# RWKV-7 recurrence and squared-ReLU FFN: stores of N and first weights on ScalarE's queue, early rounding, work dealt anew

## The chip, the cores and the metric

The kernel runs on one core of a Trainium2 chip. The metric is the device time of one execution in microseconds; several executions are taken and their median is given. The profile is of one further execution.

## The reference

Two stages follow each other. The first is a recurrence over time for each of 4 batches and 8 heads, with a 40x40 state; the second is a feed-forward layer over the 3072 rows that the first one makes.

```
for t in range(S):                       # S = 768
    y[:, :, t] = einsum('bhd,bhde->bhe', rt, state)
    Sa = einsum('bhde,bhe->bhd', state, at)
    state_decay = state * wt[:, :, None, :] - einsum('bhd,bhe->bhde', Sa, bt)
    state = state_decay + einsum('bhd,bhe->bhde', vt, kt)
x = y.transpose(0, 2, 1, 3).reshape(B * S, H * D)        # 3072 x 320
h = maximum(x @ w_in, 0.0)                               # w_in 320 x 2048
out = (h * h @ w_out).astype(float32)                    # w_out 2048 x 320
```

`r, k, v, w, a, b` are float32. The two weight matrices come as float64, and the kernel itself has to round them to float32.

## The kernel before, in words

**Chunks and slots.** Time is cut into 6 chunks of 128 steps; with 4 batches this gives 24 units of work, called chunks 0 to 23 (the batch varies fastest). The main loop has 24 slots. Slot i carries the sequential part (`chain`) of chunk i, and beside it prepares later chunks, so that each slot is a mix of several generators.

**What a chunk goes through.** `early(i)` loads nothing itself: it turns `w` on TensorE (PE), runs the decay scans and two reciprocals on VectorE (DVE), turns `b` and `a`, scales them, stores the decays (`kept_e`), multiplies them into the 128x128 matrices N, which ScalarE (ACT) copies out of PSUM (L373 to L377), and stores pieces of N to DRAM: four to `kept_q` or `kept_d`, and for chunks 2 to 23 `kept_n` and, below chunk 10, two `kept_m`. The buffer of N is single, so the next chunk's copies wait until these stores have read it. GpSimd (POOL) then loads the pieces of one unit of chunks (`take`), inverts them row by row (`solving`, L448 and L450), and stores the result to `kept_t`. `inverses(i)` (the "join") loads it back and, for chunks below 10 (`FINE` units), joins blocks of 32 into the 64-wide inverse T: a turn on DVE (L482), a copy on ACT (L484), a product on PE, a copy (L494), a second product, a copy into T (L501). `rest(i)` makes everything else that the chain of chunk i needs (`turn_k`, `make_a`, `turn_rv`, `make_rv`, `turn_down`, `scale_kb`, `turn_state`). `chain(i)` multiplies with T and N in turn, with a short ScalarE copy between the products (`xr` L619, `minus_x` L630, `xr` L637), and ends with the chunk's output (`tokens`, L669) and the new state.

**Units.** POOL solves chunks in units: 0; 1; 2, 3; 4, 5; 6, 7; 8, 9; 10, 11; and then 12 to 15, 16 to 19, 20 to 23. A unit is taken once all its chunks are prepared.

**The weights.** `fetch_weights(n, queue)` loads a float64 block of w_in or w_out (L249); blocks 0 to 2 go to three wide buffers, and later blocks are fetched when the buffer is free again. `rounding()` is a generator of 54 steps for 26 pieces; steps alternate between ScalarE (L258, L262) and VectorE (L266, L267, L275 to L277). Ten pieces of 512 columns belong to w_in, sixteen of 320 to w_out. The FFN's first product starts when w_in is rounded, its second when all of it is.

**The prologue** is written out by hand: the early parts of chunks 0 to 3 are interleaved with the first solve, with the rest and the first chain step of chunk 0, and with chunk 0's join. `go(gen, n)` runs n steps of a generator with a tick after each.

**Order.** All instructions of one engine, and all DMAs issued by it, run in program order. `store(out, in, steps)` puts a DMA into a line from which `tick()` releases it after so many ticks, on SyncE (SP) by default. `woven` (slots 0 to 3) deals generators over 12 steps; `sorted_slot` (slots 4 to 23) has an order written out by hand, with the FFN (`second`) in it. `ahead` says which chunks are prepared in which slot, `pieces_in` how many pieces are rounded in slots 0 to 3; in slot 4 the last eight steps of rounding run by `halves`. Two lines that the change touches:

```
ahead = {0: (4, 5), 1: (6, 7), 2: (8, 9), 3: (10,), 4: (11, 12), 5: (13, 14)}
pieces_in = {0: (4, TOTAL), 1: (6, TOTAL), 2: (6, TOTAL), 3: (7, TOTAL)}
```

After a pair of chunks, the tokens of some heads are moved between partitions by eight DMAs (`moves`), and `gathered` releases them for the FFN.

Of the kernel before, what the change touches and what calls it, by code (L numbers as in the profile page):

```python
# [17 lines left out]
def kernel(  # L18
# [22 lines left out]
    nc = tc.nc  # L41
    ctx.enter_context(tc.manual_schedule())
    B, H, S, D = r.shape
# [63 lines left out]
    def store(out_, in_, steps=2, queue=nc.sync):  # L107
        later(lambda: queue.dma_start(out=out_, in_=in_), steps)  # L108
# [233 lines left out]
    def early(i, g=None, apart=False):  # L342
# [36 lines left out]
        for half in range(2):  # L379
            for n in range(2):  # L380
                at = half * HC + n * Q
                if i < SMALL:
                    kept, to = kept_q[i, :, half, n], at + Q
                else:
                    u = unit_of[i]
                    kept, to = kept_d[u][i - units[u][0], :, half], (half + 1) * HC
                    kept = kept[:, n * Q * HC:n * Q * HC + Q * (to - at)].rearrange("h (s t) -> h s t", s=Q)
                store(kept.rearrange("h s t -> s h t"), t_[at:at + Q, :, at:to], 1, nc.scalar if g is not None and n else nc.sync)
            if i < SMALL and g is None:
                store(kept_m[i][half], joins(half), 1)  # L390
        if g is None:
            store(kept_n[i], t_[:HC, :, HC:], 1)
        else:
            g["dec"], g["N"] = dec, new("N21", [HC, H, HC], 2)
            nc.scalar.copy(g["N"], t_[:HC, :, HC:])
            g["joins"] = spare("joins", i)
            for half in range(2):
                nc.scalar.copy(g["joins"][half * HC:half * HC + Q], joins(half))
# [169 lines left out]
    def rest(i, g):  # L568
        begin(i, g)
        yield  # L570
        yield
        turn_k(i, g)
        joining = inverses(i, g) if i else iter(())
        if soon(i):
            next(joining, None)
        yield
        make_a(i, g)
        yield
        turn_rv(i, g)
        if i == B:  # L580
            fetch_next(i + 1, "r")
        yield
        decay_state(i, g)
        make_rv(i, g)
        if i and unit_of[i] < FINE:
            next(joining)
        yield
        turn_down(i, g)
        yield
        scale_kb(i, g)  # L590
        turn_state(i, g)
        yield
        yield from joining
        yield
# [9 lines left out]
    def chain(i, g):  # L604
# [71 lines left out]
        if n == GB - 1:  # L676
            t_ = tokens[i // GB]
            for j, row, h, d, m_ in moves:
                at = (h % 2) * DP + d
                store(t_[row:row + m_, j], t_[at:at + m_, h // 2], 1)  # L680
            later(lambda: gathered.add(i // GB), 2)
        yield


# [139 lines left out]

    e0, e1, e2, e3 = (early(i, ready[i]) if i in ready else prepare(i) for i in range(B))
    r0, first_slot = rest(0, ready[0]), chain(0, ready[0])
    go(e0, 3)
    go(e1)  # L830
# [11 lines left out]
    load_early(2)  # L842
    go(e1)
    flush()
    solve(0, {12: lambda: take(1, own)})
    go(r0)
    load_early(3)
# [1 line left out]
    go(e2, 2)  # L849
    load(1)  # L850
    go(first_slot)
    go(e2, 2)
    go(e3, 2)
    go(e2)
# [1 line left out]
    flush()  # L856
    join = inverses(0, ready[0])
    go(join)
    go(e3)
    flush()  # L860
    solve(1, {8: lambda: weights_by(0, nc.gpsimd), 20: lambda: take(2, own)})
    run(r0)
    run(join)
    weights_by(1, nc.sync)
    solve(2, {4: lambda: weights_by(2, nc.gpsimd)})
    for gen in (e0, e1, e2, e3):
        run(gen)
    flush()
# [1 line left out]


    TOTAL = 12
    ahead = {0: (4, 5), 1: (6, 7), 2: (8, 9), 3: (10,), 4: (11, 12), 5: (13, 14)}
    ahead.update({i: (i + 9,) for i in range(6, len(order) - 9)})

    pieces_in = {0: (4, TOTAL), 1: (6, TOTAL), 2: (6, TOTAL), 3: (7, TOTAL)}
    done = set(range(B))
    unit = unit_of[B]


    def woven(i, g, ch):
        jobs = [(ch, 8, 0, TOTAL)]
        made = ahead.get(i, ())
        for j, m_ in enumerate(made):
            jobs.append((prepare(m_), 5, j * 5, TOTAL - 5 * (len(made) - 1 - j)))
        if i:
            ready[i + 1] = {}
            load(i + 1, ready[i + 1])
        jobs.append((rest(i + 1, ready[i + 1]), 9, 2, TOTAL))
        m_, end = pieces_in[i]  # L890
        jobs.append((some(rounded, 2 * m_), 2 * m_, 0, end))
        weave(*jobs)
# [15 lines left out]
    def sorted_slot(i, g, ch):  # L908
# [20 lines left out]
                second.thirds()  # L929
                second.whole()  # L930

        halves = lambda: [next(rounded, None) for _ in range(2)] if not begun else None

        if more:
            begin(j, n)
        step(second.make_quarter, halves, halves)
        step(of(turn_rv), on(one), on(one), halves)
        fetch_next(j + 1, "r")
        step(second.make_quarter, halves)
        step(on(ch), of(decay_state))  # L940
        step(of(make_rv), second.thirds)
        step(on(ch), on(one), on(two), on(two))
# [25 lines left out]
    for i in range(len(order)):  # L968
# [4 lines left out]
        if i < B:  # L973
            woven(i, g, ch)
            n = ready[i + 1]
            n["chain"] = chain(i + 1, n)
            next(n["chain"])
            if i == B - 1:
                fetch_next(i + 2, "v")
                loads(i + 2)  # L980
        else:
            sorted_slot(i, g, ch)
# [37 lines left out]
```

## Time and profile before

| what | value |
|---|---|
| time, median of 3 | 987.36 us (986.25 to 987.77) |
| the profiled execution | 987.0 us, its span 985.3 us |
| PE busy | 875.7 us (89%), 8752 matmuls |
| DVE busy | 485.0 us (49%) |
| ACT busy | 275.5 us (28%) |
| POOL busy | 576.1 us (58%) |
| mean granted PE clock | 0.901 |
| DMA | 104.16 MB in 263431 packets, 246148 of them under 512 B |

The shares are means over stages with different limits. The windows view gives them stage by stage: for each stretch of time its length, the busy time and count of each engine, the granted PE clock, the share of the 16 DMA engines that is busy, and the rate. In a timeline a line reads: start in us, duration in us, engine, source line, operation, output<-input, shapes, count, and in brackets how long the engine sat idle before it and what released it. "SPq" and "ACTq" are the DMA issues on SP's and ScalarE's queues; the duration there is the issue, not the transfer.

Slots can be cut at the ScalarE copy into `xr` (L619), one for each chunk: it is written at 106.81, 156.13, 204.25, 243.42, 291.80, 337.44 and 372.81 us for chunks 1 to 7. For chunk 0 it is written in the prologue (30.91), and its first product with T starts at 65.55.

### The profile page before, as it was taken

How to read it: one execution, taken by the hardware profiler on the slowest of the kernel's cores; microseconds unless marked ns; L12 is line 12 of the kernel's file. 1: busy time of each engine (PE TensorE's matmuls, PEld its weight loads, DVE VectorE, ACT ScalarE, POOL GpSimd, SP SyncE). 2: the span in 40 equal slices, each digit the busy share in tenths (PEclk: the TensorE clock that was granted, in tenths of full speed). 3: DMA queues.
4: the chain of work that ended last, by engine and by line, in shares of the span. 5: the costliest groups of instructions: out<-in, count | busy, mean ns of one | idle time of the engine just before them, and what ended most of it. 6: DMA issues, size and time to landing. Idle time of an engine off the chain costs nothing.

```text
span 985.3 us, 21632 instructions
## 1 busy us (share of the span) xinstructions
PE 875.7 (89%) x8752; PEld 725.8 (74%) x8752; DVE 485.0 (49%) x868; ACT 275.5 (28%) x711; POOL 576.1 (58%) x989
## 2 busy tenths in 40 slices
PE   6447666667897999999999999999999999999998
PEld 4436555556685888888888888888888888887776
DVE  5528775758755454475446655632444423331111
ACT  3132423234323342332223232322222222222111
POOL 4788482836018985999976999959999800000000
PEclk9757565657698999999999999999999999999999
DMA  8987987894667579465588772585404364030000
GB/s 100 143 160 131 191 158 164 171 170 118 91 127 132 100 138 183 92 122 78 97 167 156 124 113 70 102 183 82 66 19 78 82 121 71 14 64 8 14 13 14
DMA packets 263431, 104.16 MB, mean 106 GB/s; under 512 B 246148, under 2 KB 252676, under 8 KB 261924
## 3 DMA queue, kind: packets, MB, share of 16 engines
q1 hardware_dynamic: 259188, 86.39, 50.9%
q0 software_dynamic: 3056, 16.26, 6.9%
q8 instruction: 69, 1.13, 0.5%
q10 hardware_dynamic: 1088, 0.13, 0.1%
q14 instruction: 30, 0.25, 0.1%
HBM read 70.11 MB, written 30.66 MB: 102 GB/s over the span
## 4 chain that ended last, share of the span: by engine, by line
PE 64%; SPq 1%; DVE 1%; DMA 1%; ACT 0%; issue 0%; ACTq 0%
PE ps_f L87 36%; PE ps_w L87 11%; PE ps_c L87 11%; PE ps_w L316 4%; PE ps_c L560 1%; PE ps_c L643 1%; PE ps_w L544 1%; DMA dec<-kept_e 1%; SPq L108 1%; SPq L464 0%; DMA tokens<-tokens 0%; DVE decay L357 0%; DVE state L535 0%; DVE RV L332 0%; ACT N L376 0%
## 5 line engine op out<-in xcount | busy, mean ns | idle before, releaser
L448 POOL TENSOR_TENSOR half_p<-half_n,half_t 128x120 f32<-128x120 f32 (+37 forms) x438 | 255.7, 584 | 84.4 <-DMA half_n<-kept_d 26.5
L450 POOL TENSOR_TENSOR half_t<-half_t,half_p 128x120 f32<-128x120 f32 (+37 forms) x438 | 275.9, 630 | 34.3
L87 PE MATMUL ps_f<-w_out,hid 128*128 128x320 f32 x768 | 217.4, 436 | 0.0
L87 PEld LDWEIGHTS ps_f<-w_out,hid 128*128 128x128 f32 x768 | 142.5, 190 | 54.6 <-issue 0.2
L87 PE MATMUL ps_f<-tokens,w_in 128*128 128x256 f32 x672 | 157.2, 388 | 0.0
L87 PEld LDWEIGHTS ps_f<-tokens,w_in 128*128 128x128 f32 x672 | 126.7, 194 | 17.9 <-issue 1.0
L734 DVE TENSOR_TENSOR hid<-hid 128x512 f32<-128x512 f32 x96 | 88.9, 963 | 50.2 <-ACT hid L727 49.7
L727 ACT ACTIVATE hid<-ps_f 128x512 f32<-128x512 f32 x84 | 50.2, 597 | 96.0 <-PE ps_f L87 96.0
L352 DVE TENSOR_TENSOR_SCAN decay<-ps_w,ones 128x64 f32<-128x64 f32 x88 | 23.8, 271 | 81.5 <-PE ps_w L316 81.5
L669 DVE TENSOR_TENSOR tokens<-ps_c,dec 128x512 f32<-128x512 f32 x24 | 16.5, 688 | 79.3 <-PE ps_c L87 79.3
L87 PE MATMUL ps_w<-decay,bT 40*128 40x128 f32 x352 | 30.0, 308 | 27.0 <-DVE decay L365 27.0
L373 ACT COPY N<-ps_w 128x256 f32<-128x256 f32 x48 | 17.7, 369 | 121.6 <-PE ps_w L87 74.7
L87 PEld LDWEIGHTS ps_w<-decay,bT 40*128 40x128 f32 x352 | 27.6, 213 | 30.2 <-issue 19.1
L510 DVE TENSOR_TENSOR kvT<-ps_w,dec 128x512 f32<-128x512 f32 x24 | 16.5, 688 | 66.9 <-ACT minus_x L630 33.9
L87 PE MATMUL ps_f<-tokens,w_third 64*128 64x256 f32 x336 | 46.9, 385 | 1.5 <-DVE w_out L266 1.5
L332 DVE TENSOR_TENSOR RX<-ps_w,upper 128x512 f32<-128x512 f32 x48 | 30.8, 683 | 32.1 <-PE ps_w L87 31.6
L332 DVE TENSOR_TENSOR RV<-ps_w,upper 128x512 f32<-128x512 f32 x48 | 30.9, 686 | 31.1 <-PE ps_w L87 30.8
L87 PEld LDWEIGHTS ps_c<-xr,T 64*64 64x64 f32 x768 | 30.7, 149 | 20.5 <-issue 15.0
L522 ACT COPY rT<-ps_w 128x512 f32<-128x512 f32 x24 | 14.0, 585 | 108.3 <-PE ps_w L316 108.3
L87 PE MATMUL ps_c<-xr,T 64*64 64x40 f32 x768 | 36.8, 243 | 3.6 <-ACT xr L619 1.6
L357 DVE RECIPROCAL decay<-decay 128x256 f32<-128x256 f32 x22 | 38.2, 1736 | 0.0
L532 DVE TENSOR_TENSOR f<-end,dec 128x4 f32<-128x4 f32 x20 | 5.1, 255 | 66.6 <-DMA dec<-kept_e 66.6
(130 smaller groups left out, 1411.7 us busy)
## 6 DMA issues: line engine op xcount, KB each, us to landing
kept_e<-decay SPq DMA_DIRECT2D x22, 633.8 KB
dec<-kept_e SPq DMA_DIRECT2D x22, 633.8 KB
hid<-in_moe_w_out_dram SPq DMA_DIRECT2D x16, 320.0 KB
half_n<-kept_d POOLq DMA_DIRECT2D x6, 768.0 KB, 10.3
in_w<-in_w_dram SPq DMA_DIRECT2D x24, 160.0 KB
in_ab<-in_b_dram SPq DMA_DIRECT2D x24, 160.0 KB
in_ab<-in_a_dram SPq DMA_DIRECT2D x24, 160.0 KB
in_k<-in_k_dram SPq DMA_DIRECT2D x24, 160.0 KB
```

The lines of the kernel that those rows point to most:

```text
L87: nc.tensor.matmul(o, l_, r_, start=start, stop=True, skip_group_check=True)
L316: nc.tensor.transpose(p_[:, q * 128:(q + 1) * 128], pair(x_, q), ident)
L332: nc.vector.tensor_tensor(t_, p_, over4(upper), Alu.mult)
L352: nc.vector.tensor_tensor_scan(up[:, q, MID + 1:C + 1], wT[:, q, MID:], ones, 1.0, Alu.mult, Alu.mult)
L357: nc.vector.reciprocal(down[:, :, MID + 1:C + 1], up[:, :, MID + 1:C + 1])
L373: nc.scalar.copy(plain, p_[:, ::2])
L448: nc.gpsimd.tensor_tensor(p_, part[:, at:at + m_].unsqueeze(1).to_broadcast([128, n, m_]), t3[:, :n, s:s + 1].to_broadcast([128, n, m_]), ...
L450: nc.gpsimd.tensor_tensor(t3[:, :n, s + 1:], t3[:, :n, s + 1:], p_, Alu.subtract)
L510: nc.vector.tensor_tensor(kT, kT_, down[:, :, 1:C + 1], Alu.mult)
L669: nc.vector.tensor_tensor(t_, y_, g["up"][:, :, :C], Alu.mult)
L727: nc.scalar.activation(h_, p_.rearrange("p f t -> p (f t)"), Act.Relu)
L734: nc.vector.tensor_tensor(h_, h_, h_, Alu.mult)
```

## The change

- `early`: the stores of N are no longer put into the line but issued at once, on ScalarE; only for chunks 0 and 1 does the first of each half's two pieces stay on SyncE.
- The first two weight blocks are fetched by ScalarE's queue, the first ahead of solve 0 and the second after the first chain step; the third by GpSimd inside solve 1. Before, they were fetched by GpSimd in solve 1, by SyncE after chunk 0's join, and by GpSimd in solve 2.
- Eight steps of rounding (four pieces, the last of them without its final two operations) run between the issue of the join's loads and the last step of chunk 3's early part.
- The early part of chunk 4 moves into the prologue: one step ahead of solve 1, three between and after the steps of chunk 0's join; its remaining steps run in slot 0.
- What is left is dealt anew over slots 0 to 5 (`ahead`, `pieces_in`); no rounding is left for slot 4.
- `v` of chunk 5 is fetched with `r` in slot 3 and not at that slot's end. The moves of tokens are released two ticks later.

```diff
-                store(kept.rearrange("h s t -> s h t"), t_[at:at + Q, :, at:to], 1, nc.scalar if g is not None and n else nc.sync)
+                (nc.sync if g is not None and not n else nc.scalar).dma_start(out=kept.rearrange("h s t -> s h t"), in_=t_[at:at + Q, :, at:to])
             if i < SMALL and g is None:
-                store(kept_m[i][half], joins(half), 1)
+                nc.scalar.dma_start(out=kept_m[i][half], in_=joins(half))
         if g is None:
-            store(kept_n[i], t_[:HC, :, HC:], 1)
+            nc.scalar.dma_start(out=kept_n[i], in_=t_[:HC, :, HC:])
...
         if i == B:
-            fetch_next(i + 1, "r")
+            fetch_next(i + 1, "r", "v")
...
-                store(t_[row:row + m_, j], t_[at:at + m_, h // 2], 1)
-            later(lambda: gathered.add(i // GB), 2)
+                store(t_[row:row + m_, j], t_[at:at + m_, h // 2], 3)
+            later(lambda: gathered.add(i // GB), 4)
...
-    e0, e1, e2, e3 = (early(i, ready[i]) if i in ready else prepare(i) for i in range(B))
+    e0, e1, e2, e3, e4 = (early(i, ready[i]) if i in ready else prepare(i) for i in range(B + 1))
...
     flush()
+    weights_by(0, nc.scalar)
     solve(0, {12: lambda: take(1, own)})
...
     go(first_slot)
+    weights_by(1, nc.scalar)
     go(e2, 2)
...
     go(join)
+    go(rounded, 2 * 4)
     go(e3)
     flush()
-    solve(1, {8: lambda: weights_by(0, nc.gpsimd), 20: lambda: take(2, own)})
+    go(e4)
+    solve(1, {8: lambda: weights_by(2, nc.gpsimd), 20: lambda: take(2, own)})
     run(r0)
+    go(join)
+    go(e4)
+    go(join)
+    go(e4)
     run(join)
-    weights_by(1, nc.sync)
-    solve(2, {4: lambda: weights_by(2, nc.gpsimd)})
+    go(e4)
+    solve(2)
...
-    ahead = {0: (4, 5), 1: (6, 7), 2: (8, 9), 3: (10,), 4: (11, 12), 5: (13, 14)}
-    ahead.update({i: (i + 9,) for i in range(6, len(order) - 9)})
-
-    pieces_in = {0: (4, TOTAL), 1: (6, TOTAL), 2: (6, TOTAL), 3: (7, TOTAL)}
-    done = set(range(B))
+    ahead = {0: (5,), 1: (6, 7), 2: (8, 9), 3: (10, 11), 4: (12, 13)}
+    ahead.update({i: (i + 9,) for i in range(5, len(order) - 9)})
+
+    pieces_in = {0: (5, TOTAL), 1: (6, TOTAL), 2: (6, TOTAL), 3: (6, TOTAL)}
+    done = set(range(B + 1))
...
         jobs = [(ch, 8, 0, TOTAL)]
+        if i == 0:
+            jobs.append((e4, 2, 0, 4))
...
-        halves = lambda: [next(rounded, None) for _ in range(2)] if not begun else None
...
-        step(second.make_quarter, halves, halves)
-        step(of(turn_rv), on(one), on(one), halves)
+        step(second.make_quarter)
+        step(of(turn_rv), on(one), on(one))
         fetch_next(j + 1, "r")
-        step(second.make_quarter, halves)
+        step(second.make_quarter)
...
             if i == B - 1:
-                fetch_next(i + 2, "v")
                 loads(i + 2)
```

## The prediction

> **What bounds the kernel now.** I read the windows view first, cut where ScalarE writes a slot's `xr` (106.8, 156.1, 204.3, 243.4, 291.8, 337.4, ... us): one row is one slot.
>
> ```profile
> core 0: us, PE busy (x) PEld busy (x) DVE busy (x) ACT busy (x) POOL busy (x), PEclk, DMA share, GB/s
> 0.00:65.50 65.50, 29.23 (x256) 24.09 (x256) 28.26 (x60) 16.21 (x47) 43.39 (x151) 0.78 0.91 129
> 65.50:106.80 41.30, 30.52 (x332) 26.83 (x332) 30.07 (x55) 14.85 (x41) 33.92 (x97) 0.62 0.84 150
> 106.80:156.10 49.30, 31.46 (x332) 27.69 (x332) 37.60 (x67) 17.75 (x45) 26.24 (x73) 0.60 0.88 172
> 156.10:204.30 48.20, 30.98 (x332) 26.89 (x332) 32.00 (x67) 16.07 (x46) 24.67 (x68) 0.57 0.83 166
> 204.30:243.40 39.10, 27.94 (x325) 24.04 (x326) 29.32 (x63) 14.99 (x40) 24.83 (x68) 0.63 0.75 143
> 243.40:291.80 48.40, 42.34 (x409) 36.34 (x410) 30.63 (x64) 15.70 (x39) 3.38 (x9) 0.80 0.61 106
> 291.80:337.40 45.60, 39.24 (x441) 32.89 (x442) 24.48 (x46) 13.63 (x39) 35.64 (x65) 0.93 0.69 121
> 337.40:372.80 35.40, 35.40 (x429) 29.77 (x430) 17.82 (x34) 13.73 (x39) 31.33 (x53) 1.00 0.70 130
> ```
>
> From slot 6 (337.4) on PE is busy all the time at full clock; time is to be had only in the prologue (to 65.5) and slots 0 to 5. There no engine is full: the slot is a relay of VectorE, PE at 0.6 clock and loads. The timelines of PE show which wait ends last:
>
> ```profile
> 170.15 1.11 PE L316 MATMUL ps_w<-ident,in_k 128*128 128x128 f32 x4 [5.55 <-DMA in_k<-in_k_dram]
> ...
> 177.80 1.08 PE L316 MATMUL ps_w<-ident,in_w 128*128 128x128 f32 x4 [4.53 <-DMA in_w<-in_w_dram]
> ...
> 248.82 1.09 PE L316 MATMUL ps_w<-ident,in_v 128*128 128x128 f32 x4 [4.40 <-DMA in_v<-in_v_dram]
> ...
> 255.31 2.17 PE L87 MATMUL ps_f<-tokens,w_third 64*128 64x256 f32 x7 [1.53 <-DVE w_out L266]
> ...
> 312.80 1.08 PE L316 MATMUL ps_w<-ident,in_w 128*128 128x128 f32 x4 [5.93 <-DMA in_w<-in_w_dram]
> ```
>
> The loads are late because SP's queue issues everything in order. At slot 2's start, in SP's timeline, tokens (5.34 us) and seven stores of N (from 154.83 to 160.97) stand ahead of `in_k` (161.73). VectorE's timeline of the prologue shows the one large hole, 20.34 us before it turns chunk 0's blocks:
>
> ```profile
> 61.49 0.45 DVE L482 STREAM_TRANSPOSE spares<-blocks 128x256 f32<-128x256 f32 x1 [20.34 <-DMA blocks<-kept_t]
> ```
>
> **What the Trainium skill says.** "DMA: Bandwidth & Descriptors", section "Issuing engines are not separate DMA queues": transfers of all issuers run on the same 16 engines, and a second issuer saves sequencer time only. The trace agrees: at 22.2 us two ScalarE stores took 1.89 us beside an SP load of 1.98 us. "TensorE: Matmul & The Clock Gate", section "What's actually happening": the clock is half by default, and full after some 3.4 us of sustained work. Here, too: 0.57 to 0.63 in slots 0 to 3, 1.00 from slot 6; the sixteen `w_in` products after the wait at 312.8 took 5.34 us, those at 328.5 took 3.62.
>
> **The change, part by part** (minus is a gain).
>
> *Stores of N.* Four `kept_q`/`kept_d`, up to two `kept_m` and one `kept_n` go to ScalarE: seven per chunk below 10, five after. Median issues of the same stores on SP: 0.52, 0.59, 0.56 us, and 0.43 for `kept_d`; so 3.8 us for seven, 2.3 for five. They come at once after the copies of N, ahead of what ScalarE does next. At a slot's end that is the join:
>
> ```profile
> 152.07 0.26 ACT L377 COPY N<-ps_w 64x128 f32<-64x128 f32 x1
> 152.35 0.75 ACT L494 COPY spares<-ps_w 32x256 f32<-32x256 f32 x2
> 154.31 0.73 ACT L501 COPY T<-ps_w 32x256 f32<-32x256 f32 x2 [1.20 <-PE ps_w L87]
> 156.13 0.42 ACT L619 COPY xr<-ps_c 128x320 f32<-128x320 f32 x1 [1.09 <-PE ps_c L87]
> ```
>
> L494 follows the last copy at once, PE waits for L494, `xr` for PE: the issues lie on the path. So +3.5 (rounded down, ScalarE's four issues of before had a median of 0.43) at the ends of slots 0, 1, 2 and +2.3 at slot 3's, and about +1 in mid-slot for the other chunk, where rounding queues behind the stores and VectorE for it. Both ends: 0 (the join is late anyway) to 10 us per slot end (seven at 1.46, the longest ScalarE issue seen).
> From slot 6 on there is one chunk per slot to slot 14. In slot 8 the copies end at 435.5; `sd` and two relus end by 437.9, the next thing PE needs is `xr` at 441.65, after 3.69 us of idle. 2.3 us fit: 0 taken, +1 per slot (nine slots) at worst, nothing to gain as PE is full.
>
> *SP relieved.* Some 6 us per chunk leave SP's queue; tokens (two ticks later) go behind the next loads. So the waits shown go: slot 0 its 1.1 for `in_w` and 1.4 of a wait for `kept_n` to free N; slot 1 3.25 of PE's wait for `in_w` at 125.8; slot 2 6.5 of 10.1 (the two above; the data still needs its time on engines that are 0.83 busy); slot 3 3.6 (VectorE's wait for `dec`). Bounds: none of it, or another 4 per slot.
>
> *`v` of chunk 5 fetched one slot earlier.* The 4.40 us at 248.8 go. SP sat idle 7.5 us ahead of 234, so the issue (0.61) costs nothing.
>
> *Four pieces rounded in the prologue.* A 512-column piece is five VectorE operations of 0.68 (3.4 us), a 320-column one 2.5. Four take 13.6 us in program order ahead of L482; the hole is 20.3. They need fetches 0 and 1 (1 MB each), now issued by ScalarE near 24 and 32 us, and landed by about 45 if POOL's 5.8 us from issue to landing grows to twice that. The 2 MB pass over engines that were at a share above 1 from 20 to 51 us, so chunks 2 and 3 come some 2 us later. ScalarE's eight issues (4 us) are hidden by the wait for T until 61. What is late next is chunk 3's N, which now queues on ScalarE behind the rounding: near 54 instead of 51, its stores until 60, just ahead of L484. POOL has its four weight issues moved within a busy stretch, 0.
>
> *Chunk 4's early part in the prologue.* Eight scans, two reciprocals, two products: 1.5+3.4+1.3 = 6.2 us of VectorE, most of it beside the join's PE and ScalarE steps. PE's eight transposes (1.97 at half clock) stand ahead of the join's second product, where it waited 0.75 for ScalarE: +1.2. Blocks land about 1 us sooner, as fetch 0 is out of their way. Prologue in sum +0.5; -1.5 to +5.
>
> *Dealt anew.* Slot 0: one early part out (-6.2), one piece in (+3.4): -2.9. Slots 1, 2: as before. Slot 3: chunk 11 in (+6.2), one piece less (-2.5): +3.7. Slot 4: no rounding, so 1.5 of PE's wait at 255.3 goes, and with both waits gone the clock rises sooner than 262.6; PE worked some 13 us at half clock there, a third of it at full saves 4. Slot 5 prepares one chunk, like slot 6, whose `in_w` was loaded a slot earlier: the wait of 5.93, chunk 13's PE work (2.7) and some 2 at half clock after the wait go. I let it come to slot 6's length, 35.4: -10.2.
>
> Sum by slot: prologue +0.5; slot 0 -2.9-2.5+3.5+1 = -0.9; slot 1 -3.25+4.5 = +1.2; slot 2 -6.5+4.5 = -2; slot 3 +3.7-3.6+3.3 = +3.4; slot 4 -4.4-1.5-4+1 = -8.9; slot 5 -10.2. Total **-16.9**, taken as -16. The profiled run took 987.0 (span 985.3), 0.4 below the median of 987.36; so about **971**.
>
> *POOL* could take the gain back: its solves run without a gap from 286 to 786, and T of chunk 20 was loaded at 790.3, 4.3 us after its solve. But unit 6 (chunks 10, 11) is complete a slot earlier, so that chain starts some 45 us sooner, and then waits for N of chunks 15, 19 and 23, which move with the slots. Units take 136 us, and from N of chunk 23 (633) to the use of T of chunk 20 (793) there are 160. Cost 0.
>
> **The rivals.** (a) *ScalarE becomes the bound*, slower: in slots 0 to 3, with DMA share 0.75 to 0.88, issues stall as the 1.46 us one did. Slot ends then cost 10.2 three times and 7.3, mid-slots 3 each: 50 instead of my 16.8, so -16 becomes +17: about 1004. It decides from an issue of about 1.0 us, where the extra 33 are half reached. Against it: medians of 0.43 to 0.59; for it: SP's mean for `kept_q` is 0.80. Nearer values give 988 to 996. (b) *The work is only moved*: slots 0 to 3 and the prologue lose what slot 4 and 5 win, since the transfers there fill the engines and a relieved SP gains nothing: my 16 us of freed waits outside slots 4 and 5 shrink to 4, so about 983. (c) *Stores hidden*: the join waits for its blocks anyway and slot ends cost nothing: 12.8 us less, 958. (d) The rounding finds its weights late and holds L482: prologue +5 to +10, 977 to 981.
>
> **How the numbers follow.** Mine 0.42, (b) 0.15, (c) 0.13, (d) 0.12, (a) 0.18, half of it above 994. Range 955 to 994: it leaves out the bad half of (a) and the edge of (c). A difference under 0.2% (2 us) is about what a measurement of this kernel can't tell from none. Faster 0.77, same 0.06 (between b and a), slower 0.17.
>
> **What would show it.** Right: `in_k`, `in_v`, `in_w` waits of PE gone from slots 2, 4, 5; slot 5 near 36; four roundings between 40 and 60; ScalarE DMA issues between L377 and L494 of 2 to 4 us; PE full from slot 5. Wrong: slot ends with 6 us or more of ScalarE issues; L482 later than 63; PE idle after 337 beside POOL or `xr`.

## The result and the profile after

The change made the kernel slower: **1019.34 us median (1015.64 to 1020.8, 4 runs)** against 987.57 us for the kernel before (4 runs), a ratio of **1.032 (1.0286 to 1.0351)**. The profiled execution, the shortest of the four, took 1015.64 us; its span is 1013.9: 28.6 longer than before, where I had forecast 16.9 shorter.

The windows view of the kernel after, cut at the same events as before's (first product with T, then each `xr` at L619), has one row for the prologue and one for each of slots 0 to 5:

```profile
core 0: us, PE busy (x) PEld busy (x) DVE busy (x) ACT busy (x) POOL busy (x), PEclk, DMA share, GB/s
0.00:85.30 85.30, 32.15 (x269) 26.14 (x269) 45.69 (x90) 20.42 (x55) 46.92 (x160) 0.76 0.85 142
85.30:135.10 49.80, 29.79 (x320) 25.99 (x320) 28.64 (x50) 16.73 (x43) 30.11 (x90) 0.57 0.67 141
135.10:188.80 53.70, 31.80 (x332) 27.93 (x332) 32.99 (x67) 16.05 (x46) 26.57 (x73) 0.60 0.70 143
188.80:236.00 47.20, 31.79 (x332) 27.85 (x332) 31.70 (x67) 15.67 (x46) 22.93 (x64) 0.57 0.75 147
236.00:282.90 46.90, 34.34 (x353) 29.81 (x354) 31.60 (x67) 15.82 (x45) 24.76 (x68) 0.57 0.66 113
282.90:331.10 48.20, 38.76 (x409) 33.70 (x410) 24.36 (x45) 12.98 (x32) 36.28 (x69) 0.88 0.60 119
331.10:366.60 35.50, 35.50 (x429) 29.86 (x430) 20.11 (x36) 13.70 (x40) 31.73 (x49) 1.00 0.58 103
```

The prologue is 19.7 us longer and slot 0 8.6; slot 5 is as short as forecast. The work is the same over the span (VectorE 485.5 us against 485.0, ScalarE 275.5 in both); VectorE's 17.4 us more in the prologue are chunk 4 and the four pieces moved into it. The DMA engines were less busy in slots 0 to 3 than before (0.67, 0.70, 0.75, 0.66 against 0.84, 0.88, 0.83, 0.75). So what grew is waiting. The first fence is from VectorE's list of waits up to 135 us, the next three from PE's in slot 0, in slots 1 to 3, and in slots 3 and 4 (total us, times, longest); the last is from PE's list for slots 1 to 3 of the kernel **before**:

```profile
DVE ps_f L277 <- ACT w_in L262: 17.5, 1, 17.5
```
```profile
PE ps_c L87 <- ACT xr L637: 5.9, 1, 5.9
PE ps_w L87 <- ACT spares L494: 4.4, 1, 4.4
```
```profile
PE ps_w L87 <- DVE decay L365: 21.3, 6, 4.5
PE ps_w L87 <- ACT spares L494: 20.5, 3, 9.9
```
```profile
PE ps_w L316 <- DMA in_w<-in_w_dram: 8.9, 1, 8.9
```
```profile
PE ps_w L87 <- DVE decay L365: 14.5, 3, 6.0
PE ps_w L316 <- DMA in_w<-in_w_dram: 7.8, 2, 4.5
PE ps_w L316 <- DMA in_k<-in_k_dram: 6.0, 2, 5.6
PE ps_w L87 <- ACT spares L494: 5.7, 3, 2.1
```

PE's waits for `in_k` and `in_w` in slots 1 to 3 (6.0 and 7.8 us before) are gone, as forecast; but PE's three waits for the join's copy L494 there grew from 5.7 us to 20.5, and those for VectorE's L365 by 6.8. Most of what grew waits for ScalarE, which has no more work than before. Its timeline in the prologue shows what holds it. "ACTq" are its DMA issues; where a line merges several (x2, x4), the second number runs from the start of the first to the end of the last, with what lies between:

```profile
29.26 2.67 ACTq L249 DMA_DIRECT2D w_out<-in_moe_w_in_dram  x2
31.96 0.59 ACT L522 COPY rT<-ps_w 128x512 f32<-128x512 f32 x1 [7.83 <-DMA kept_q<-N]
...
38.78 10.35 ACTq L249 DMA_DIRECT2D w_out<-in_moe_w_in_dram  x4
49.23 0.37 ACT L373 COPY N<-ps_w 128x256 f32<-128x256 f32 x1 [10.03 <-DMA in_b<-in_b_dram]
...
50.99 0.33 ACTq L388 DMA_DIRECT2D kept_q<-N  x1
...
55.86 0.35 ACTq L388 DMA_DIRECT2D kept_q<-N  x1
57.83 0.67 ACTq L390 DMA_DIRECT2D kept_m<-N  x1
58.59 1.24 ACTq L388 DMA_DIRECT2D kept_q<-N  x2
65.67 0.57 ACTq L390 DMA_DIRECT2D kept_m<-N  x1
66.33 0.57 ACTq L392 DMA_DIRECT2D kept_n<-N  x1
66.95 0.66 ACT L262 ACTIVATE w_in<-w_out 128x512 f32<-128x512 uint32 x1 [15.43 <-DMA kept_q<-N]
```

Read the releasers in brackets: an ordinary copy (L522, L373) is "released" by a DMA whose data it never touches. The issue that stands ahead of the copy was waiting for that DMA. The issues themselves are short up to here, 0.3 to 0.7 us, but **between** them are holes. A semaphore is a counter that an instruction can wait for. The trace names for each DMA the semaphore that it counts up when it lands, when it landed, and what its issue waits for. In this kernel SyncE and ScalarE draw theirs from the same eight semaphores. Each of the prologue's seven long holes stands ahead of an issue that waits for the very semaphore that it will count up, and ends 0.021 to 0.022 us after the landing of the transfer that had it last:

| issue by ScalarE | hole before it, us | its semaphore was last taken by |
|---|---|---|
| weights, 29.26 | 5.12 | a piece of the same weight block, ScalarE |
| weights, 31.62 | 2.07 | `kept_q`, SyncE |
| weights, 43.98 | 4.77 | `in_r`, SyncE |
| weights, 48.83 | 4.16 | `in_b`, SyncE |
| `kept_q`, 55.86 | 4.33 | `in_ab`, SyncE |
| `kept_m`, 57.83 | 1.62 | `kept_e`, SyncE |
| `kept_m`, 65.67 | 5.84 | `blocks`, SyncE |

That is 27.9 us in which ScalarE, which works in order, could start nothing else. In slots 0 to 3 such holes come to no more than 1.1, 1.8, 0.4 and 0.6 us. There the issues themselves stand ahead of the join: from a slot end's first store to L494 it is 4.2, 8.7, 4.7 and 3.3 us. ScalarE's timeline at the end of slot 1:

```profile
176.29 0.31 ACTq L388 DMA_DIRECT2D kept_q<-N  x1
...
177.82 2.56 ACTq L388 DMA_DIRECT2D kept_q<-N  x2
180.42 2.16 ACTq L390 DMA_DIRECT2D kept_m<-N  x1
184.42 0.55 ACTq L392 DMA_DIRECT2D kept_n<-N  x1
185.01 0.75 ACT L494 COPY spares<-ps_w 32x256 f32<-32x256 f32 x2 [8.19 <-DMA kept_q<-N]
```

One hole of 1.84 us is in it, but two issues alone take 1.68 and 2.16. The fourteen of slot 1 take 12.8 us and those of slot 2 10.2, against 7.2 in slot 0; what makes some of them long was not settled.

In the prologue, L522 comes at 31.96 (24.11 before), chunk 2's copies of N at 49.23 (36.65), the first rounding at 66.95, chunk 0's turn L482 at 78.79 (61.49) and its first product with T at 85.3 (65.6).

### The profile page after: what moved, and what is told of

It reads as the page before. It is cut to its first block, busy times and chain, and to the rows that moved or that the text cites. A ratio compares the mean times of both kernels' runs of the same rounds, so it can differ in the third digit from the quotient of the medians.

```text
span 1013.9 us, 21580 instructions
## 1 busy us (share of the span) xinstructions
PE 877.5 (87%) x8752; PEld 728.0 (72%) x8752; DVE 485.5 (48%) x868; ACT 275.5 (27%) x711; POOL 576.1 (57%) x985
## 4 chain that ended last, share of the span: by engine, by line
PE 74%; DVE 8%; DMA 6%; ACT 3%; ACTq 3%; issue 2%; POOL 2%; SPq 1%; DVEq 0%; POOLq 0%
PE ps_f L87 39%; PE ps_w L87 14%; PE ps_c L87 13%; PE ps_w L316 5%; ACTq L388 1%; DMA kept_q<-N 1%; DVE decay L357 1%; PE ps_c L643 1%; DMA blocks<-kept_t 1%; PE ps_c L560 1%; DMA in_w<-in_w_dram 1%; PE ps_w L544 1%; ACT N L376 1%; DVE ps_f L275 1%; SPq L108 1%
## 5 line engine op out<-in xcount | busy, mean ns | idle before, releaser
L87 PEld LDWEIGHTS ps_f<-tokens,w_in 128*128 128x128 f32 x672 | 125.6, 192 | 17.5 <-issue 1.0
L734 DVE TENSOR_TENSOR hid<-hid 128x512 f32<-128x512 f32 x96 | 90.5, 979 | 50.2 <-ACT hid L727 49.7
L727 ACT ACTIVATE hid<-ps_f 128x512 f32<-128x512 f32 x84 | 49.1, 599 | 82.5 <-PE ps_f L87 82.5
L332 DVE TENSOR_TENSOR RV<-ps_w,upper 128x512 f32<-128x512 f32 x48 | 30.9, 685 | 63.1 <-PE ps_w L87 63.0
L87 PE MATMUL ps_w<-decay,bT 40*128 40x128 f32 x352 | 32.1, 326 | 27.9 <-DVE decay L365 24.4
L87 PEld LDWEIGHTS ps_w<-decay,bT 40*128 40x128 f32 x352 | 29.6, 231 | 30.8 <-issue 16.8
L87 PE MATMUL ps_w<-rT,kvT 40*128 40x128 f32 x384 | 33.0, 317 | 17.4 <-ACT kvT L523 14.3
L373 ACT COPY N<-ps_w 128x256 f32<-128x256 f32 x48 | 17.7, 368 | 105.3 <-PE ps_w L87 90.4
L87 PE MATMUL ps_f<-tokens,w_third 64*128 64x256 f32 x336 | 45.6, 378 | 0.5 <-ACT hid L727 0.5
L332 DVE TENSOR_TENSOR RX<-ps_w,upper 128x512 f32<-128x512 f32 x48 | 30.8, 684 | 30.3 <-PE ps_w L87 29.7
L420 POOL DMA_DIRECT2D half_n<-kept_q x14 | 7.3, 528 | 66.4 <-DMA kept_q<-N 39.3
L522 ACT COPY rT<-ps_w 128x512 f32<-128x512 f32 x24 | 14.0, 585 | 108.3 <-PE ps_w L316 100.4
```

The lines of the kernel that those rows point to most:

```text
L87: nc.tensor.matmul(o, l_, r_, start=start, stop=True, skip_group_check=True)
L332: nc.vector.tensor_tensor(t_, p_, over4(upper), Alu.mult)
L373: nc.scalar.copy(plain, p_[:, ::2])
L522: nc.scalar.copy(g["rT"], p_)
L727: nc.scalar.activation(h_, p_.rearrange("p f t -> p (f t)"), Act.Relu)
L734: nc.vector.tensor_tensor(h_, h_, h_, Alu.mult)
```

## The experiments

**Theory 1:** a ScalarE DMA waits for the landing of whichever transfer last had its semaphore, SyncE's included, and holds ScalarE's copies behind it. **Theory 2:** transfers fill the DMA engines, so that issues are slow. **Theory 3:** the rounding ahead of L482 makes the prologue long. Below, T0 is the first product with T and "slots" are slots 0 to 5 of the profiled execution, us:

| run | T0 | slots 0 to 5 |
|---|---|---|
| before | 65.6 | 41.3 49.3 48.1 39.2 48.4 45.6 |
| after | 85.3 | 49.9 53.7 47.2 46.9 48.2 35.4 |
| `w_pool` | 82.7 | 58.5 52.0 46.8 45.9 48.5 36.1 |
| `stores_sp` | 77.4 | 44.0 45.4 47.7 44.7 47.2 35.4 |
| `w_pool_stores_sp` | 71.3 | 49.7 44.3 47.4 44.1 48.4 35.4 |
| `deal_only` | 61.4 | 44.3 50.2 50.3 45.7 56.3 35.4 |
| `before_act_stores` | 59.9 | 60.5 54.3 47.2 38.3 49.2 40.8 |
| `act_stores_later` | 82.7 | 46.8 45.0 56.1 44.6 50.0 35.5 |
| `v_and_tokens` | 62.3 | 45.4 50.1 49.6 39.2 47.7 45.8 |
| `stores_sp_load13` | 75.3 | 41.4 44.2 48.4 45.2 38.1 35.4 |
| `no_rounding_ahead` | 84.8 | 52.4 59.7 47.6 47.6 48.5 36.1 |
| `stores_sp_load13_no_ahead` | 74.9 | 40.4 48.1 48.6 45.2 39.6 35.4 |
| `weights_pool_load13` | 68.6 | 56.9 43.3 47.7 44.9 39.3 35.4 |
| `deal_load13_v_tokens` | 61.3 | 45.3 51.3 49.3 45.4 46.3 35.4 |

Executions of the same prologue differ: before, `deal_only`, `v_and_tokens` and `deal_load13_v_tokens` have T0 at 65.6, 61.4, 62.3 and 61.3. Single stages are read to 2 to 4 us only. The ratios below are to the kernel before measured beside each run, with medians of 989.64 to 989.91 us.

**`stores_sp`** is the change with the stores of N back in SyncE's line.

```diff
-                (nc.sync if g is not None and not n else nc.scalar).dma_start(out=kept.rearrange(...), in_=...)
+                store(kept.rearrange(...), ..., 1, nc.scalar if g is not None and n else nc.sync)
-                nc.scalar.dma_start(out=kept_m[i][half], in_=joins(half))
+                store(kept_m[i][half], joins(half), 1)
-            nc.scalar.dma_start(out=kept_n[i], in_=t_[:HC, :, HC:])
+            store(kept_n[i], t_[:HC, :, HC:], 1)
```

> The changed kernel, but the stores of N go back to SP's queue with their old delay; weights still by ScalarE. Theory 1: the 15.4 us that ScalarE stood between the copies of chunk 2's N and its first rounding go, so the prologue shortens by 10 to 15 us (first product with T at 70 to 75), and each of slots 0 to 3 loses the ScalarE issues at its end (4.4 us of PE's wait in slot 0, up to 9.9 and 6.2 in slots 1 and 2): time 985 to 995. Theory 2: only the slot ends change, prologue stays at 85: 1000 to 1008. Theory 3: as theory 2.

985.95 us, ratio to before 0.9972 (0.9945 to 0.9998). This one edit takes back the whole loss: 25.4 us between the profiled spans, some 34 by the two ratios (the change's profiled execution was its shortest, this one's 4.2 above its median). Prologue and slots 0, 1 and 3 give it (7.9, 5.9, 8.3, 2.2). ScalarE still stands for 17.5 us in five holes ahead of weight issues.

**`before_act_stores`** is the converse: the kernel before with only those stores at once on ScalarE.

> The kernel before, with only the stores of N moved to ScalarE and issued at once. Theory 1 (a ScalarE store waits for the landing of the transfer that last used its completion semaphore, and what ScalarE does next waits behind it): clearly slower, by 8 to 30 us: each of slots 0 to 2 longer by 3 to 10 us, the prologue by up to 10, and ScalarE's DMA issues show gaps that end within 0.1 us of such a landing. Rival (issue time alone, 0.5 us each): 3.8 us per slot end, 10 to 15 us in all, without gaps. If the stores are harmful only together with the weights and the rounding ahead: within 5 us of before.

1006.73 us, ratio 1.0165 (1.0131 to 1.02). Slot 0 grows from 41.3 to 60.5. PE's list of waits from 60 to 250 us (slots 0 to 3) again names ScalarE:

```profile
PE ps_w L87 <- ACT spares L494: 19.9, 3, 9.6
PE ps_w L87 <- ACT kvT L523: 12.6, 3, 10.2
PE ps_c L87 <- ACT xr L637: 7.6, 3, 6.7
```

Here there are no weights on ScalarE and no new rounding, so neither is needed for a loss, and the holes are there: 10.1 us of them in slot 0. But T0 is 59.9: ahead of it nothing is lost, so what the change loses there needs the weights, too. Slot 6 alone is 9.2 us longer (44.6 against 35.4): a store `kept_d` stands 4.9 us for its semaphore, the copy into T (L501) comes behind it, and PE waits for that:

```profile
365.46 1.04 PE L87 MATMUL ps_c<-xr,T 64*64 64x40 f32 x16 [3.38 <-ACT T L501]
```

In the 14 us after it PE's granted clock is 0.63; before, it is 1.00 in all of slot 6.

**`act_stores_later`** keeps the stores on ScalarE, but releases them from the line a tick later instead of at once.

```diff
-            nc.scalar.dma_start(out=kept_n[i], in_=t_[:HC, :, HC:])
+            store(kept_n[i], t_[:HC, :, HC:], 1, nc.scalar)
```
(and so for `kept_q`, `kept_d` and `kept_m`)

> The changed kernel, but the stores of N, still on ScalarE, go through the line with a delay of one tick, so that they come behind what ScalarE does in the same step (join, rounding). If the order at the slot ends is what costs (L494 behind seven stores): 8 to 15 us less than the changed kernel, 1004 to 1011, with PE's wait for L494 back under 3 us. If the waits for semaphores cost wherever the stores stand: the prologue still has its first product with T at 80 or later, and the time falls by less than 8 us: 1011 to 1019.

1015.65 us, ratio 1.0247 (1.0204 to 1.0291). Some slots gain and slot 2 loses 9; T0 is still 82.7. PE's waits for L494 are down to 5.7 us from 60 to 250 us, but it waits for other copies of ScalarE instead (L637 9.4, L523 8.2, L619 7.6). By the ratios 7 of the 34 us come back: it is the engine that issues, more than the place in the slot, that costs.

**`w_pool`** and **`w_pool_stores_sp`** give the first two weight blocks to GpSimd; the second also takes the stores of N back to SyncE.

```diff
-    weights_by(0, nc.scalar)
-    solve(0, {12: lambda: take(1, own)})
+    weights_by(0, nc.gpsimd)
+    solve(0, {4: lambda: weights_by(1, nc.gpsimd), 12: lambda: take(1, own)})
...
-    weights_by(1, nc.scalar)
```

> The changed kernel, but GpSimd issues weight blocks 0 and 1 (block 0 at the same place ahead of solve 0, block 1 at step 4 inside solve 0). Theory 1: in the prologue ScalarE stands still at its own DMA issues, because each waits until an earlier transfer that uses the same completion semaphore (101 to 108, shared with SP) has landed. GpSimd uses eight others (111 to 118), so ScalarE's waits of 5.1, 2.1, 4.9 and 4.2 us between weight issues go, rT is written near 25 us instead of 32, the copies of chunk 2's N near 38 instead of 49. The stores of chunk 2's N still wait, so the first product with T moves from 85.3 to 68 to 74, and the time from 1019 to 1003 to 1008. Theory 2 (the 2 MB crowd the DMA engines, whoever issues them): prologue and time stay within 3 us. Theory 3 (rounding and chunk 4's early part simply stand ahead of the join): stay, too.

> Both: weights 0 and 1 by GpSimd and stores of N on SP; rounding ahead, chunk 4's early part in the prologue, the new deal, v and tokens stay as in the changed kernel. Theory 1: no DMA of ScalarE is left but four; the prologue is back to 65 to 68, slot 5 stays at 35.5: time 970 to 980, below the kernel before. Theory 2: 2 MB still in the prologue, first product with T at 75 or later, time over 988. Theory 3: rounding holds the turn of chunk 0's blocks: first product with T at 72 or later.

1019.85 us, ratio 1.031 (1.0285 to 1.0334), and 991.13, ratio 1.000 (0.9987 to 1.0012). Both are misses: I had expected T0 at 68 to 74 and at 65 to 68, and nothing lost elsewhere. With the weights gone ScalarE copies chunk 2's N earlier (44.65 in `w_pool`), but its stores still have holes (47.01 to 59.52 for seven), and the blocks come late. GpSimd now issues before it solves (chunk 0's result is stored at 57.21, in the change at 48.19), and SyncE's loads of it, four issues, take 13.44 us. The first fence is SyncE's timeline, the second ScalarE's:

```profile
61.86 13.44 SPq L470 DMA_DIRECT2D blocks<-kept_t  x4
```
```profile
77.59 0.91 ACT L484 ACTIVATE T<-blocks,which 128x256 f32<-128x256 f32 x2 [7.40 <-DMA blocks<-kept_t]
```

The second of the four stands 10.70 us and goes out at 73.27, 0.016 us after ScalarE's store `kept_q` of 69.65 has landed, which had its semaphore. So SyncE, too, is held by a transfer of the other engine that it shares no data with, here right ahead of T0. Theory 2 had expected `w_pool` within 3 us of the change, in T0 and in time, and so it is; but what holds T0 there is this wait, not slow issues.

In `w_pool_stores_sp` T0 falls by 6.1 beside `stores_sp`, and slot 0 gives 5.7 back: PE waits 9.9 us for `in_w` there, and ScalarE 10.5 for `kept_n` to free N. What the weights cost on ScalarE comes back in slot 0 when GpSimd issues them.

**`no_rounding_ahead`** is the change with no rounding ahead of the join (theory 3).

```diff
-    go(rounded, 2 * 4)
-    pieces_in = {0: (5, TOTAL), 1: (6, TOTAL), 2: (6, TOTAL), 3: (6, TOTAL)}
+    pieces_in = {0: (6, TOTAL), 1: (7, TOTAL), 2: (7, TOTAL), 3: (7, TOTAL)}
```

> The change without the four pieces rounded ahead of chunk 0's join (they go to slots 0 to 3). Theory 1 (waits for semaphores hold ScalarE's copies): VectorE turns chunk 0's blocks once they have landed, near 68 instead of 78.8, chunk 0's first product with T comes at 74 to 76 instead of 85.3; slots 0 to 3 get 1 piece each more, +1.5 to 3 each; total 1012 to 1018: of the prologue's 19.7 us some 10 are the rounding that was held by late stores, the others ScalarE's own waits. Theory 3 (the rounding alone makes the prologue long): the first product comes by 66 and the total is under 1008. If the weights' and stores' waits hold the blocks anyway, the first product stays past 82 and the total at 1019.

1024.5 us, ratio 1.0352 (1.0327 to 1.0376); T0 84.8. L482 did come early, at 69.67, but ScalarE's next step of the join did not. Its timeline:

```profile
73.27 0.37 ACT L373 COPY N<-ps_w 128x256 f32<-128x256 f32 x1 [21.04 <-DMA kept_n<-N]
...
78.88 1.74 ACTq L390 DMA_DIRECT2D kept_m<-N  x1
80.71 0.71 ACTq L392 DMA_DIRECT2D kept_n<-N  x1
81.47 0.91 ACT L484 ACTIVATE T<-blocks,which 128x256 f32<-128x256 f32 x2 [5.91 <-DMA kept_q<-N]
```

Chunk 2's last store of N went out only at 69.11, so chunk 3's copies waited 21 us for the buffer, and its seven stores stand ahead of L484. Theory 3 falls, and so does my own split of the prologue: of the alternatives on record the last held. In the change two chains end together, the rounding (L482 at 78.79) and chunk 3's stores (L484 at 81.97 right behind them), and both begin after chunk 2's late stores.

**`deal_only`** is the kernel before with the new `ahead` alone, **`v_and_tokens`** with `v` and the tokens alone.

```diff
-    ahead = {0: (4, 5), 1: (6, 7), 2: (8, 9), 3: (10,), 4: (11, 12), 5: (13, 14)}
-    ahead.update({i: (i + 9,) for i in range(6, len(order) - 9)})
+    ahead = {0: (4, 5), 1: (6, 7), 2: (8, 9), 3: (10, 11), 4: (12, 13)}
+    ahead.update({i: (i + 9,) for i in range(5, len(order) - 9)})
```

> The kernel before with the deal alone: chunk 11 prepared in slot 3, chunks 12 and 13 in slot 4, one chunk per slot from slot 5 on; prologue, stores, weights and rounding as before. If the prediction's step for the deal was right: slot 5 from 45.6 to about 35.5, slot 3 longer by 4 to 8, slot 4 shorter or the same: time 978 to 985. If the wait of PE for in_w only moves from slot 5 to slot 4 (the changed kernel shows one of 8.9 us there): 985 to 990.

> The kernel before, with v of chunk 5 fetched in slot 3 and the moves of tokens two ticks later, nothing else. The prediction's step: PE's wait of 4.4 us for in_v in slot 4 goes, waits for in_k in slot 2 shrink: 978 to 985. If another load is late in its place: 985 to 990.

993.75 us, ratio 1.0042 (1.0027 to 1.0056), and 988.17, ratio 0.9977 (0.9965 to 0.9989). The dealing takes 10.2 from slot 5 and gives 6.5 to slot 3 and 7.9 to slot 4: a slightly slower kernel. PE waits 3.4 us for `in_w` in slot 3 and 8.0 in slot 4. The early `v` removes its wait of 4.4 from slot 4, but PE's wait for the rounding there (L266) grows from 1.5 to 4.8, and only 2 us of time come of it.

**`stores_sp_load13`** asks whether slot 4's loss is only that load: `stores_sp`, and chunk 13's `w`, `b` and `a` loaded at the end of slot 3.

```diff
             if i == B - 1:
+                load_early(3 * B + 1)
                 loads(i + 2)
```

> The changed kernel with the stores of N on SP (as in stores_sp) and, in addition, the inputs of chunk 13 loaded at the end of slot 3 and not when slot 4 starts to prepare chunk 12. PE's wait of 8.9 us for in_w in slot 4 should go: slot 4 from 47.2 to 39 to 41 and the time from 986 to 977 to 980. If slot 4 is bound elsewhere (VectorE, clock), 2 us or less come.

**979.37 us, ratio 0.9884 (0.9852 to 0.9915)**: faster than both kernels, and by one line faster than `stores_sp`. Its windows view for slot 4 and PE's list of waits from 225 to 331 us:

```profile
254.50:292.60 38.10, 37.88 (x411) 33.10 (x410) 22.93 (x46) 12.87 (x32) 13.44 (x34) 0.95 0.85 168
```
```profile
PE ps_w L316 <- DMA in_w<-in_w_dram: 2.0, 1, 2.0
```

Slot 4 falls from 47.2 to 38.1 at a clock of 0.95, with PE nearly always busy: the 9.9 us that I had forecast for its dealing were there, behind one late load.

**Three versions around it.** `stores_sp_load13_no_ahead` also drops the rounding ahead; `weights_pool_load13` gives the weights to GpSimd inside the solves and rounds two pieces ahead; `deal_load13_v_tokens` is the kernel before with the dealing, `v`, the tokens and the early load, its prologue untouched.

```diff
 weights_pool_load13, beside stores_sp_load13
-    weights_by(0, nc.scalar)
-    solve(0, {12: lambda: take(1, own)})
+    solve(0, {12: lambda: take(1, own), 20: lambda: weights_by(0, nc.gpsimd)})
-    weights_by(1, nc.scalar)
-    go(rounded, 2 * 4)
+    go(rounded, 2 * 2)
-    solve(1, {8: lambda: weights_by(2, nc.gpsimd), 20: lambda: take(2, own)})
+    solve(1, {8: lambda: weights_by(1, nc.gpsimd), 20: lambda: take(2, own)})
-    solve(2)
+    solve(2, {4: lambda: weights_by(2, nc.gpsimd)})
-    pieces_in = {0: (5, TOTAL), 1: (6, TOTAL), 2: (6, TOTAL), 3: (6, TOTAL)}
+    pieces_in = {0: (6, TOTAL), 1: (6, TOTAL), 2: (6, TOTAL), 3: (7, TOTAL)}
```

> The stores of N in SyncE's line, chunk 13's w loaded a slot early, and no rounding ahead of the join. If the rounding ahead pays even with the stores back (it fills VectorE's hole), this is slower than 979 by the work that slots 0 to 3 get: 982 to 988. If the rounding is what keeps the first product with T at 75 instead of 62 to 66, the prologue falls by 5 to 10 and slots 0 to 3 gain 6 to 10: 975 to 982, no difference that matters.

> The stores of N in SyncE's line, chunk 13's w loaded a slot early, the weight blocks issued by GpSimd inside the solves of chunks 0, 1 and the next unit, two pieces rounded ahead. Theory 1: with no 1 MB block issued by ScalarE no long wait stands ahead of its copies, the first product with T comes at 63 to 68 (75.3 with the blocks on ScalarE), slots 0 to 3 get 1 piece more in three of them (+1.5 to 3 each): 968 to 977. If GpSimd's late issue makes the rounding wait for its data and hold VectorE's turn of the blocks, the prologue stays at 72 to 76 and the total at 980 to 986.

> The kernel before with the new dealing of chunks (chunk 11 in slot 3, 12 and 13 in slot 4, one a slot from 5 on), v of chunk 5 and the tokens as in the change, and chunk 13's w loaded a slot early; prologue, weights, rounding and stores of N as before. If the parts add up: the dealing alone was 4.0 us slower than before, the early w takes the wait of 8 us for it (and some 6 at half clock) from slot 4, v another 4: 974 to 982. If PE's waits in slots 3 and 4 only move to what is late next (ScalarE's and VectorE's relay), 984 to 990.

981.67 us (ratio 0.992, 0.9896 to 0.9945), 983.71 (0.9943, 0.9927 to 0.9958) and 981.95 (0.9918, 0.9895 to 0.9942). Without the rounding ahead T0 is 74.9 instead of 75.3: the four pieces do lie in VectorE's hole at no cost once the stores are off ScalarE, but what they save is small. T0 stays near 75 with the weights still on ScalarE. Chunk 2's copies of N are late by it, SyncE's stores of N follow them, and the join's loads stand behind these in SyncE's queue: issued at 62.06 in `stores_sp_load13_no_ahead` and at 54.34 before, though the solve had ended by 49.5 in both. `weights_pool_load13` clears that (T0 68.6) but rounds on data that have not come. In slot 0 VectorE waits for a weight block, and PE for VectorE, as their lists of waits up to 130 us show:

```profile
DVE ps_f L275 <- DMA hid<-in_moe_w_in_dram: 16.6, 1, 16.6
```
```profile
PE ps_w L316 <- DVE A L332: 16.6, 1, 16.6
```

Slot 0 is 56.9, and the total misses the 968 to 977 that I had hoped for. `deal_load13_v_tokens` has most of the gain with the old prologue: in sum the rearranged prologue is worth little or nothing (the intervals of 0.9918 and 0.9884 overlap). What pays differs. There it is mostly slot 5, with 10.2 us; slot 4, still with rounding in it, is 46.3, and PE waits 4.8 us for L266. Where no rounding is left in slot 4, it is 38.1 and 39.6, and that makes up for the longer prologue.

**The wait by itself.** In `count_of_eight` and `ninth_transfer` nothing of the reference is computed. They have seven stages of loads, of which this is the core (`ninth_transfer` also has ScalarE copy something first):

```
for m_ in range(count):                       # loads of 1 MB
    loads_by.dma_start(out=big[m_], in_=rows[...])
small_by.dma_start(out=small, in_=...)        # one load of 10 KB
```

> No part of the reference is computed: seven stages, each of K loads of 1 MB by one engine and then, by another engine and with nothing in the data to wait for, one load of 10 KB. Pairs: SyncE 4, 7, 8, 10 then ScalarE; GpSimd 8 then ScalarE; SyncE 8 then GpSimd; SyncE 8 then ScalarE. Theory 1 (SyncE's and ScalarE's transfers take eight completion semaphores in turn): with 4 and 7 ScalarE's load is issued at the stage's start; with 8 it is the ninth and is issued within 0.1 us after the stage's first 1 MB load has landed, 5 us or more into the stage; with 10 after the third has landed; behind GpSimd's loads, and by GpSimd behind SyncE's, at once. Theory 2 (a ScalarE issue is slow when the DMA engines are full): the issue is stretched in all stages alike, growing with K, behind GpSimd's loads too.

> No part of the reference is computed: seven stages, each begun when everything of the stage before has landed. In each, one engine issues K loads of 1 MB; ScalarE copies for about 4 us and then issues one load of 10 KB into a tile that nothing else has touched. SyncE with K = 12, 4, 8, 10, 12; then GpSimd with K = 12; then SyncE with 12. Theory 1: with 4 ScalarE's load goes out right behind its copies; with 10 and 12 behind SyncE's it goes out later, within 0.1 us after a load of SyncE's has landed, the one that last used its semaphore; behind GpSimd's 12 it goes out right behind the copies. SyncE's own ninth load waits for its first in the same way. Theory 2 (full DMA engines slow the issue itself): it goes out right behind the copies each time and takes longer, with 12 of either engine.

The first tested nothing on ScalarE: from its second stage on, the small load overwrote a tile that VectorE still had to read, so it was not free to go. The second showed the sharing, from the other side. SyncE's list of waits from 70 to 113 us, in stages whose buffers had all been free since the stage began:

```profile
SPq L59 <- DMA big<-in_moe_w_in_dram: 10.7, 7, 2.3
SPq L59 <- DMA small<-in_r_dram: 1.7, 2, 1.0
```

SyncE's load of its own 1 MB tile waits for **ScalarE's** 10 KB load, which it shares nothing with but a semaphore: the two go out at 79.54 and 108.35, 0.016 us after the small load has landed. Within a stage of 12, SyncE's later loads wait for its own first ones in the same way (0.017 us after their landings). GpSimd's loads from the ninth on wait for GpSimd's own first ones, on eight other semaphores. ScalarE's load itself never waited, which I had expected with 10 and 12: it went out some 2.7 us into the stage, and its semaphore had been free for 15 us or more. With four to ten of the 1 MB loads issued ahead of it its issue took 0.47 to 0.54 us, so a busy DMA alone did not slow it; the long issues of slots 1 and 2 in the change are left unexplained. The test did not force a hole on ScalarE. That ScalarE's holes are such waits is read in the traces of the full kernels, from what each issue waits for and when that landed; what they cost, from `stores_sp` and `before_act_stores`.

## Why the prediction was wrong

Two steps failed. The prediction put the waits ahead of ScalarE's issues at nothing, and the prologue took 19.7 us more instead of 0.5; and it took the relief of SyncE as a gain of 15.85 us in slots 0 to 3, where no gain is to be seen. `stores_sp` splits the difference in two, between profiled executions. The stores' part is the cost on ScalarE less the relief of SyncE; the rest is everything else:

| | stores, forecast | stores, measured | rest, forecast | rest, measured |
|---|---|---|---|---|
| prologue | 0 | +7.9 | +0.5 | +11.9 |
| slot 0 | +2.0 | +5.9 | -2.9 | +2.7 |
| slot 1 | +1.25 | +8.3 | 0 | -3.9 |
| slot 2 | -2.0 | -0.5 | 0 | -0.4 |
| slot 3 | -0.3 | +2.2 | +3.7 | +5.5 |
| slot 4 | +1 | +1.0 | -9.9 | -1.2 |
| slot 5 | 0 | 0 | -10.2 | -10.2 |
| from slot 6 | 0 | +0.7 | 0 | -1.2 |
| sum (measured: of the spans) | +2.0 | +25.4 | -18.8 | +3.2 |

By the medians the stores' part is some 34 us and the rest -2.8 (ratio 0.9972).

- **Stores of N: wrong.** The step "3.8 us for seven" priced each DMA by its issue. By their medians the issues were as priced (0.47, 0.46, 0.59 and 0.53 us for `kept_q`, `kept_d`, `kept_m`, `kept_n`), and slot 0's end shows it well: seven stores from 127.15 to 131.31, L494 at 131.36. Missing is the wait ahead of an issue. In the prologue seven stores took 15.9 us, and in the sum I gave them nothing there. At the ends of slots 0 to 3 there are few such waits: 20.9 us instead of 12.8, most of the difference in slot 1, where issues were long. Rival (a) had the direction, and 1004. Its long issues are there in part (a mean of 0.91 us in slot 1, 0.73 in slot 2), but the prologue's loss, which it did not have, comes of holes of up to 5.8 us between short ones. (Its 16.8 us of mine count four mid-slots; my sum by slot has five, 17.8. Nothing hangs on it.)
- **SyncE relieved: the waits went, the gain was wrong.** The waits for `in_k` and `in_w` in slots 1 to 3 went, 13.8 us; PE's waits for L494 there grew by 14.8, and those for L365 by 6.8. A load that comes sooner was worth nothing where the join came later. With the stores back on SyncE (`stores_sp`) those waits for loads are there again, 13.7 us, and slots 0 to 3 are 15.9 us shorter.
- **Weights in the prologue: wrong.** "now issued by ScalarE near 24 and 32 us, and landed by about 45": they were issued until 49.1. I asked when the data come, and not what ScalarE could do meanwhile. With the weights on ScalarE and the stores back, T0 is 75 to 77, with neither of them there 71.3, before 61 to 66. ScalarE issued four DMAs in the trace of before, too few to show it. Such a wait in SyncE's queue is in that trace, and I had not looked for it: at 65.29 us a weight issue follows a hole of 1.81 and the landing of a `kept_q` by 0.016.
- **The Trainium skill's sentence was read too widely.** "DMA: Bandwidth & Descriptors", section "Issuing engines are not separate DMA queues", promises a saving of sequencer time to a second issuer. No run here contradicts that of SyncE; what it costs the engine that issues is not in it. The two long issues at 22.2 us that I read as agreement show only that two issues can be long at once.
- **Rounding ahead: right only with the stores off ScalarE.** Then it fits VectorE's hole at no cost (T0 75.3 with it, 74.9 without).
- **Slot 4: wrong.** `v` and the rounding step went as forecast (4.4 and 1.5 us of PE's waits gone), and the clock rose. But the wait for `in_w` that I took out of slot 5 came back in slot 4, with 8.9 us: chunk 13 is now prepared there, and its `w` is loaded only when chunk 12 is begun. I had looked for the wait where one chunk is left and not where the second one went. `stores_sp_load13` removes it, and slot 4 gives 10.3 beside before.
- **Slot 3: mis-sized.** I set +3.7 for chunk 11 (less one piece) against -3.6 for VectorE's wait for `dec`. That wait fell to 0.9 in `deal_only` and to nothing in `stores_sp` and in the change. But the slot got 6.5 longer in `deal_only` and 5.5 in `stores_sp`: the sum had VectorE's work for chunk 11 in it, but not PE's, which was busy 3.5 and 6.6 us longer there at a granted clock of 0.65 and 0.58. New are also waits of VectorE for PE's products (L332), 4.7 and 3.8 us. No single one of these accounts for the slot.
- **Slot 5, slots from 6 on and POOL: right.** 45.6 to 35.4 as forecast, for the reason given; from slot 6 on 647.4 us against 647.9. That the stores cost nothing there is in part luck: in `before_act_stores` one of them meets a taken semaphore, and slot 6 loses 9.2. (GpSimd's solves before were not "without a gap": from 286 to 786 us it waits 26.5 for its own loads. The conclusion stands.)
- **Left open.** Why some issues of slots 1 and 2 are long. And slot 0 of `stores_sp` is +2.7 and not -2.9. Up to there `stores_sp_load13` is the same program, and had 41.4 instead of 44.0, so most of this may be the spread between executions.

## What to carry to other kernels

A DMA moved to another engine costs that engine the issue and every wait that stands ahead of it. Where two engines draw on the same completion semaphores, each can be held by a slow transfer of the other (ScalarE for 22.8 of its 27.9 us in the change's prologue, SyncE for 10.7 in `w_pool`), and a compute engine that works in order holds all its copies meanwhile. Look in the timeline for ordinary copies released by a DMA whose data they do not read. When work is dealt anew, follow each load to the slot where its user now stands: one line that issued a load a slot earlier took `stores_sp` from 0.9972 to 0.9884 of before.

## What the runs showed of the hardware

- In these programs SyncE's and ScalarE's DMAs take turns on eight completion semaphores, GpSimd's on eight others. An issue that finds its semaphore taken follows the landing of the transfer that had it by 0.016 to 0.022 us on SyncE and ScalarE in the holes read here, and by 0.284 on GpSimd in `ninth_transfer`.
- The holes are long for small transfers too: ScalarE's store `kept_m` at 65.67 stood 5.84 us for one 32 KB load of `blocks`.
- In two prologues that differ only in the rounding ahead, the granted clock of PE up to 61 us was 0.71 (`stores_sp_load13_no_ahead`) and 1.00 (`stores_sp_load13`), and T0 was 74.9 and 75.3: PE's clock did not set T0 there.
